# Parity of a long convolution's inner index on the partitions' halves, and two second stages in 64x64 blocks

## The chip, the cores and the metric

The kernel runs on one core of one Trainium2 chip. The metric is the device time of one launch in microseconds (us). The kernel before takes 2227.91 us, the median of three runs (2227.91, 2227.91 and 2229.37).

## The reference

Two layers follow one another. The first is a long convolution (a Hyena filter): with x and v of 4 batches x 12544 positions x 128 channels,

```python
h_filt = (np.maximum(pos_emb @ w1, 0.0) @ w2) * exp(-0.01 * pos)[:, None]
u  = x * v
y  = irfft(rfft(u, 2S) * rfft(h_filt, 2S))[:, :S]
x2 = x * y
```

The second is a feed-forward layer with a maximum of three products, `h = max(x2 @ w1, x2 @ w2, x2 @ w3)` and `h @ w_out`, with 128 channels and 768 hidden ones. All is fp32; the weights of the second layer arrive as 64-bit floats and are turned into fp32 on VectorE.

## The kernel before, in words

The transform of the convolution is split by hand into matrix products. A position is a block index (98 blocks for the signal, NH = 82 for the filter, whose window is zero after that) and an index s2 of 0 to 127 within the block. The **first stage** is a product over the blocks, which gives N1 = 90 complex frequencies for each s2 and channel. The **second stage** is a product over s2 with twiddles, frequency pair by frequency pair (NK = 45 pairs, called g). Signal and filter are then multiplied, and a third and a fourth product lead back. s2 is always split by its parity r: 2t+r with t of 0 to 63.

The work runs in four blocks of time. The instructions are issued in the order in which the program writes them (a manual schedule), one queue per engine, so an instruction that waits holds all that stands behind it on its engine.

**Loading and the filter's small network** (to 39.6 us). `pos_emb` is loaded in eight DMAs (L315) as two halves of the blocks (h = 0: blocks 0 to 40, h = 1: blocks 41 to 81) on two halves of the partitions. `mlp_in` (L346) multiplies by w1, `mlp_out` (L358) takes the maximum with zero and the window on VectorE and writes `hs`, which has 105 partitions: 41 blocks from partition 0 and 41 from partition 64. Between them stand the products of the first signal groups.

**First stages** (39.6 to 111.6 us). The loop over f (L1036) makes the first stage of the filter's 64 inner channels in 16 quads of four channels. `quad` calls `first_halves` (L170): for each channel, for each parity r and each half c of the table (real and imaginary part) one matmul of 105 partitions x 64 columns of weights x 90 columns, 16 per quad, and one ScalarE copy of 720 elements from PSUM into `specH`. Beside them VectorE multiplies x by v for signal groups 4 to 7 (`u_mul`, L384), TensorE turns them (`turn2`, L977), and `some` (L963) issues pieces of `convert` (L227), the 12 VectorE steps by which half of a weight matrix is turned from 64-bit floats into fp32; there are 8 such halves. `load_raw` (L214) fetches the next half by four DMAs on GpSimd's queue. After the 16 quads GpSimd copies four parts of the signal's spectrum that had been put `aside` (L1048), because `hs` lay on their place. Then the loop over u (L1050) does the same for signal groups 4 to 31, two at a time: two `quad`s of group u and u+1, one `turn2` of groups u+4 and u+5, and the loads (L379, on SyncE's queue) of u+10 and u+11. A `turn2` needs both products x*v of its groups. The PSUM tiles of this block are four, `acc`, taken in turn.

**The loop over frequency pairs of batch 0** (L1174, 111.6 to 279.6 us, NK + 3 = 48 steps). Step s holds:

- `s_second` (L1104): the filter's second stage, 4 matmuls of 128 x 64 x 128 columns into a PSUM tile of its own, and a ScalarE copy of 128 elements;
- `g_second` (L608): the signal's, 8 matmuls of 128 x 64 x 128 into another tile, and a ScalarE copy of 256 elements (`evens`);
- for the step before: `g_swap` (two ScalarE copies L627, L628) and `s_filter` (L1125), 16 matmuls of 64 x 64 x 128 that bring in w2, and a ScalarE copy of 1024 elements (L1151);
- for three steps before: `g_third` (L649), 8 matmuls of 128 x 64 x 128, a ScalarE copy (L660) and a store;
- for two steps before: the store of the filter's spectrum (`s_store`, on GpSimd's queue), the complex product `g_re`, `g_im` (two multiplications on VectorE, L633 and L637, and an addition on GpSimd, L638);
- for this step: `s_sums` (L1117, two sums of 128 elements on VectorE) and `butterfly` (L195, two sums of 256), both of even and odd parity;
- last on VectorE, `g_unfold` (L641, two sums L645), which waits for GpSimd's addition.

**Batches 1 to 3 and the second layer** (from 279.6 us). This fills the rest. The change does not touch it.

Of the kernel before, what the change touches and what calls it, by code (L numbers as in the profile page):

```python
# [42 lines left out]
def tables(NB):  # L43
# [11 lines left out]
    f1h = np.zeros((64 + HH, 2, 2 * N1))  # L55
    f1h[:HH, 0], f1h[64:, 0] = f1[:HH], f1[HH:NH]
    f1h[:HH, 1], f1h[64:, 1] = f1[HH:NH], f1[:HH]
# [11 lines left out]
    fwd = np.stack(half, 2)  # L69
# [26 lines left out]
def kernel(  # L96
# [53 lines left out]
    f1_sb = const.tile([NB, 2 * N1], FP32, name="f1")  # L150
    f1 = f1_sb[:]
# [18 lines left out]
    def first_halves(ps, lhs, table, dsts, engines):  # L170


        for i, a in enumerate(lhs):
            for r in range(2):
                for c in range(2):
                    nc.tensor.matmul(  # L176
                        ps[64 * c:64 * c + 64, 256 * i + r * N1:256 * i + (r + 1) * N1],
                        a[:, r, :], table[r][:, c * N1:(c + 1) * N1],
                        start=(i % 2 == 0 and r == 0), stop=True, skip_group_check=True)
        v = ps[:].rearrange("p (s m) -> p s m", m=256)[:, :, 0:2 * N1].rearrange(  # L180
            "p s (r k) -> p k r s", r=2)
        k0 = 0
        for dst, copy in zip(dsts, engines):
            k1 = k0 + dst.shape[1]
            copy(dst, v[:, k0:k1])
            k0 = k1

    def second(ps, w, g):

        for k in range(2):  # L190
            for r in range(2):
                halves_mm(ps[:, (2 * k + r) * D:(2 * k + r + 1) * D], w[:, k, r, :],
                          spec[:, 2 * g + k, r, :], k == 0 and r == 0, True)

    def butterfly(ps, eo, xs):  # L195
        v = ps[:, :].rearrange("p (k r d) -> p k r d", k=2, r=2)
        nc.vector.tensor_tensor(out=xs[:, :, 0, :], in0=eo[:], in1=v[:, :, 0, :], op=ALU.add)
        nc.vector.tensor_tensor(out=xs[:, :, 1, :], in0=eo[:], in1=v[:, :, 0, :],
                                op=ALU.subtract)

    def evens(ps, eo):
        v = ps[:, :].rearrange("p (k r d) -> p k r d", k=2, r=2)
        nc.scalar.copy(eo[:], v[:, :, 1, :])

# [19 lines left out]
    def convert(r, i, h):  # L227
# [6 lines left out]
        one = nc.vector.tensor_single_scalar  # L234
        tt = nc.vector.tensor_tensor
        ONE = 0x3F800000
# [3 lines left out]
            lambda: two(out=f2_, in0=lo, scalar1=9, scalar2=ONE,  # L240
                        op0=ALU.logical_shift_right, op1=ALU.bitwise_or),
            lambda: two(out=f1_, in0=hi, scalar1=12, scalar2=9,
                        op0=ALU.logical_shift_left, op1=ALU.logical_shift_right),
            lambda: one(f1_, f1_, ONE, op=ALU.bitwise_or),
            lambda: two(out=ex, in0=hi, scalar1=1, scalar2=21,
                        op0=ALU.logical_shift_left, op1=ALU.logical_shift_right),
            lambda: two(out=ex, in0=ex, scalar1=896, scalar2=0,
                        op0=ALU.subtract, op1=ALU.max),
            lambda: one(ex, ex, 255, op=ALU.min),
            lambda: one(ex, ex, 23, op=ALU.logical_shift_left),  # L250
            lambda: two(out=sg, in0=hi, scalar1=31, scalar2=31,
                        op0=ALU.logical_shift_right, op1=ALU.logical_shift_left),
            lambda: tt(out=ex, in0=ex, in1=sg, op=ALU.bitwise_or),
            lambda: one(f1f, f1f, 2.0 ** -20, op=ALU.subtract),
            lambda: nc.vector.scalar_tensor_tensor(
                out=f1f, in0=f2f, scalar=2.0 ** -20, in1=f1f, op0=ALU.mult, op1=ALU.add),
# [28 lines left out]
    w1_sb = sml.tile([P, FO], FP32, name="w1_sb")  # L285
    w2_in = sml.tile([P, D], FP32, name="w2_in")
# [10 lines left out]
    f1h = sml.tile([64 + HH, 2, 2 * N1], FP32, name="f1h")  # L297
# [6 lines left out]
    for h in range(2):  # L304
        nc.gpsimd.dma_start(
            win[64 * h:64 * h + HH],
            window[0, h * HH * P:(h + 1) * HH * P].rearrange("(n p) -> n p", p=P))
# [5 lines left out]
    for j, (lo_, hi_) in enumerate(zip(cuts, cuts[1:])):  # L313
        for h in range(2):
            (nc.scalar if (h + j) % 2 else nc.sync).dma_start(  # L315
                pos[64 * h:64 * h + 64, lo_ * P:hi_ * P],
                posT[:, (h * HH + lo_) * P:(h * HH + hi_) * P])
# [290 lines left out]
    def g_second(g):  # L608
        ps = state["cv"][1].tile([P, 512], FP32, tag="cv", name="ps2")
        second(ps, ws.pop((g, 0)), g)  # L610
        eo = state["cv"][0].tile([P, 2, D], FP32, tag="eo", name="eo", bufs=2)
        evens(ps, eo)
        pss[g], eos[g] = ps, eo

    def g_butterfly(g):
        if g % 3 == 2:
            xt = specH[:, 0:4].rearrange("p k r f -> p (k r f)").rearrange(
                "p (k r d) -> p k r d", k=2, r=2)
        else:
            xt = state["cv"][0].tile([P, 2, 2, D], FP32, tag="x", name="xt", bufs=state["xb"])  # L620
        butterfly(pss.pop(g), eos.pop(g), xt)
        xts[g] = xt

    def g_swap(g):
        xt = xts[g]
        xs = state["cv"][0].tile([P, 2, 2, D], FP32, tag="xs", name="xs", bufs=2)
# [3 lines left out]

    def g_re(g):
        xt = xts[g]
        nc.vector.tensor_tensor(out=xt[:], in0=xt[:], in1=hts[g][0][:], op=ALU.mult)  # L633

    def g_im(g, apart=False):
        xt, xs = xts[g], xss.pop(g)
        nc.vector.tensor_tensor(out=xs[:], in0=xs[:], in1=hts.pop(g)[1][:], op=ALU.mult)  # L637
        (nc.gpsimd if apart else nc.vector).tensor_tensor(  # L638
            out=xt[:], in0=xt[:], in1=xs[:], op=ALU.add)

    def g_unfold(g):  # L641
        y = xts.pop(g)
        ab = state["cv"][0].tile([P, 2, 2, D], FP32, tag="ab", name="ab", bufs=2)
# [756 lines left out]
```

## Time and profile before

| | |
|---|---|
| time, median of 3 runs | 2227.91 us |
| time of the profiled execution | 2221.21 us |
| its span, first to last instruction | 2219.4 us |
| granted TensorE clock, mean | 0.997 |
| TensorE matmul busy | 2194.1 us, 99% |
| VectorE busy | 1534.6 us, 69% |
| ScalarE busy | 1210.9 us, 55% |
| GpSimd busy | 1179.0 us, 53% |
| filter's first stage (16 quads and 2 turns) | 39.6 to 61.7 us |
| signal's first stage, groups 4 to 31 | 61.7 to 111.6 us |
| loop of batch 0 | 111.6 to 279.6 us |

How to read it: a time in the trace is counted from the start of the span. PE is TensorE's matmuls, PEld its weight loads, DVE VectorE, ACT ScalarE, POOL GpSimd, SPq SyncE's queue of DMA issues. The trace has two records for each fp32 matmul, so 16 matmuls show as x32. A busy TensorE is one that always had a matmul in flight; whether it was held up by others is seen only from what each engine waited for. L12 is line 12 of the kernel before.

### The profile page before, as it was taken

Reading aid. Unit: us, or ns where it says so; the run is one execution under the profiler, and the core shown is the slowest. Engines: PE = TensorE matmul, PEld = TensorE weight load, DVE = VectorE, ACT = ScalarE, POOL = GpSimd, SP = SyncE. Lnnn points to the kernel's source line nnn. Section 1 sums busy time; section 2 is a strip of 40 time slices with the busy share of each in tenths; the row PEclk is TensorE's granted clock in tenths of the full one; section 3 lists DMA queues with packets and bytes.
Section 4 is the critical chain, followed back from the end, with each engine's and each line's share of the span. In section 5 each row is a group of like instructions: output and inputs, shape, how many; then the busy total and the mean of one; then the engine's idle time right before and its main releaser. Section 6 shows DMA issues by size and latency. Waiting matters only on the chain.

```text
span 2219.4 us, 77166 instructions
## 1 busy us (share of the span) xinstructions
PE 2194.1 (99%) x31655; PEld 1297.3 (58%) x31655; DVE 1534.6 (69%) x3293; ACT 1210.9 (55%) x2223; POOL 1179.0 (53%) x1577
## 2 busy tenths in 40 slices
PE   9999999999999999999999999999999999999999
PEld 7988755555555455555555555555555545667776
DVE  5688857677877766667888766677878744554443
ACT  3699845466666555456666555556666622222222
POOL 1166567534455566544444566634454426666665
PEclk9999999999999999999999999999999999999999
DMA  8789999879999898879999999969999722222221
GB/s 196 186 264 311 291 181 196 171 191 233 247 246 241 218 188 175 168 175 245 230 256 231 229 195 178 173 158 252 236 240 238 200 79 58 59 71 69 63 58 24
DMA packets 491332, 411.62 MB, mean 185 GB/s; under 512 B 289406, under 2 KB 407920, under 8 KB 490979
## 3 DMA queue, kind: packets, MB, share of 16 engines
q1 hardware_dynamic: 443689, 274.50, 56.6%
q0 software_dynamic: 45808, 130.25, 21.5%
q8 instruction: 249, 4.08, 0.8%
q10 hardware_dynamic: 1482, 1.93, 0.4%
q14 instruction: 104, 0.85, 0.1%
HBM read 262.85 MB, written 84.67 MB: 157 GB/s over the span
## 4 chain that ended last, share of the span: by engine, by line
PE 84%; DMA 6%; DVE 3%; POOL 3%; issue 2%; SPq 1%; ACT 1%; POOLq 0%; DVEq 0%; ACTq 0%
PE hps L167 42%; PE ops L167 17%; PE ops L903 6%; PE cps L167 3%; PE cps L449 3%; PE ps L176 3%; PE cps L547 3%; PE cps L557 2%; DMA sq<-spec 2%; DMA ht<-hd 2%; DMA zt<-zd 1%; PE ps L167 1%; DMA wt<-wq_const 1%; POOL xt L638 1%; PE last L167 1%
## 5 line engine op out<-in xcount | busy, mean ns | idle before, releaser
L167 PE MATMUL hps<-gt,w_sb 128*64 128x392 f32 (+1 forms) x7672 | 1157.4, 495 | 0.8 <-DVE gt L829 0.7
L839 ACT ACTIVATE hid<-hps 128x392 f32<-128x392 f32 x768 | 382.5, 498 | 762.7 <-PE hps L167 744.9
L167 PEld LDWEIGHTS hps<-gt,w_sb 128*64 128x64 f32 (+1 forms) x7672 | 430.6, 126 | 439.1 <-issue 407.9
L842 DVE TENSOR_TENSOR hid<-hid,hps 128x392 f32<-128x392 f32 x768 | 427.8, 557 | 351.5 <-PE hps L167 335.8
L167 PE MATMUL ops<-hid,wo_sb 128*64 128x392 f32 x2304 | 476.9, 492 | 0.0
L599 POOL TENSOR_TENSOR cb<-cb,xs 128x512 f32<-128x512 f32 x135 | 177.4, 1314 | 404.9 <-DVE xs L596 389.5
L167 PEld LDWEIGHTS ops<-hid,wo_sb 128*64 128x64 f32 x2304 | 165.7, 137 | 213.5 <-issue 213.5
L572 DVE TENSOR_TENSOR cb<-cps,eo 128x512 f32<-128x512 f32 (+1 forms) x288 | 175.1, 649 | 72.8 <-ACT eo L569 71.7
L857 POOL DMA_DIRECT2D out_dram<-ot x96 | 76.3, 795 | 235.3 <-ACT ot L855 217.2
L587 ACT ACTIVATE xs<-cb 32x512 f32<-32x512 f32 x270 | 169.4, 628 | 21.5 <-DVE cb L572 12.6
L588 ACT COPY xs<-cb 32x512 f32<-32x512 f32 x270 | 166.3, 616 | 3.2
L603 DVE TENSOR_TENSOR xs<-cb 128x256 f32<-128x256 f32 x270 | 148.7, 598 | 6.5 <-POOL cb L599 6.5
L429 ACT COPY uT<-turned 113x512 uint16<-113x512 uint16 x180 | 126.0, 771 | 0.1
L386 POOL TENSOR_TENSOR ut<-ut 128x392 f32<-128x392 f32 x90 | 93.3, 1037 | 41.2 <-DMA ut<-in_vr_dram 39.2
L167 PEld LDWEIGHTS cps<-f4p,even 90*64 90x64 f32 x1552 | 87.2, 138 | 35.9 <-issue 33.2
L772 POOL DMA_DIRECT2D xT<-in_x_dram x172 | 101.1, 601 | 6.8 <-PE pt L1099 3.3
L580 POOL DMA_DIRECT2D zd<-cb x135 | 95.0, 704 | 14.6 <-DVE cb L572 10.7
L471 DVE TENSOR_TENSOR low<-high,cps 128x180 f32<-128x180 f32 x186 | 54.6, 334 | 67.6 <-ACT high L461 67.6
L928 POOL DMA_DIRECT2D out_dram<-o x120 | 72.5, 610 | 47.2 <-DVE o L921 45.7
L167 PE MATMUL cps<-f4p,zt 90*64 90x49 f32 x1552 | 95.8, 222 | 0.0
L547 PE MATMUL cps<-sq,wt 64*64 64x128 f32 x2160 | 90.6, 276 | 4.6 <-DMA wt<-wq_const 2.9
L413 POOL COPY planes<-ut 128x392 uint16<-128x392 uint16 x180 | 95.1, 564 | 0.0
(172 smaller groups left out, 3348.2 us busy)
## 6 DMA issues: line engine op xcount, KB each, us to landing
ht<-hd SPq DMA_DIRECT2D x264, 256.0 KB, 7.1
wt<-wq_const POOLq DMA_DIRECT2D x144, 256.0 KB, 5.3
zd<-cb POOLq DMA_DIRECT2D x135, 256.0 KB, 6.3
zt<-zd SPq DMA_DIRECT2D x384, 90.0 KB, 3.8
sq<-spec SPq DMA_DIRECT2D x528, 64.0 KB, 5.6
ut<-in_xr_dram SPq DMA_DIRECT2D x128, 196.0 KB, 4.3
ut<-in_vr_dram SPq DMA_DIRECT2D x128, 196.0 KB, 4.5
wt<-wt_const SPq DMA_DIRECT2D x90, 256.0 KB, 5.1
```

The lines of the kernel that those rows point to most:

```text
L167: nc.tensor.matmul(out[h:h + w], lhsT[:, h:h + w], rhs, start=start, stop=stop, skip_group_check=True)
L429: nc.scalar.copy(uts[u][0:HR, 8 * (u % 2):8 * (u % 2) + 8].rearrange("n s r t -> n (s r t)").bitcast(U16).rearrange("n (s r t h) -> n h s ...
L547: nc.tensor.matmul(ps[64 * a:64 * a + 64, at:at + D], w[64 * r:64 * r + 64, k, a, :], t[64 * r:64 * r + 64, k, :, a], start=(k == 0), stop ...
L572: nc.vector.tensor_tensor(out=cb[:, a, lo:hi], in0=ps[:, lo:hi], in1=eo[:, lo:hi], op=op)
L587: nc.scalar.mul(xs[at:at + 32], xt[at + 32:at + 64], -1.0)
L588: nc.scalar.copy(xs[at + 32:at + 64], xt[at:at + 32])
L599: nc.gpsimd.tensor_tensor(out=xts[g], in0=xts[g], in1=xs[:], op=ALU.add)
L603: nc.vector.tensor_tensor(out=ab[:, q], in0=y[:, 0], in1=y[:, 1], op=(ALU.subtract, ALU.add)[q])
L772: eng.dma_start(xT[c * NG:(c + 1) * NG].rearrange("d i p n -> d (i p) n"), x[:, 4 * i:4 * i + 8, c, b, :])
L839: nc.scalar.activation(h[:], pa[:, 0:N], Relu)
L842: nc.vector.tensor_tensor(out=h[:], in0=h[:], in1=pb[:, 0:N], op=ALU.max)
L903: nc.tensor.matmul(ps[32 * q:32 * q + 32, 0:H2], w[:, m:m + 32], rhs[:, H2 * c:H2 * c + H2], start=start, stop=True, skip_group_check=True)
```

## The change

Everything touches the first two blocks after loading and the loop of batch 0.

- `first_halves` now takes both halves of the table in one matmul (180 columns) and puts the parity r on the partitions' halves of the result: 8 matmuls per quad in place of 16. `spec` so holds r, not real and imaginary part, on its halves.
- The filter's quads are replaced by `filter_halves`. Its rows are now split by the parity p of the block index (partition 0: even blocks, partition 64: odd blocks; the loads of `pos_emb` and the window follow, in runs of 128 elements). Each half is multiplied apart, in 16 matmuls of 41 x 64 x 90, into the two banks of a PSUM tile. The sum and the difference of the two banks are the frequencies of both kinds. ScalarE copies one bank (360 elements) and VectorE makes both, or, in every second quad (`apart`), ScalarE copies both (720), VectorE makes the sum and GpSimd the difference. `eo` has one buffer for each of the two sizes.
- `u_mul` of the first and the second block moves from VectorE to GpSimd.
- `convert` has 10 VectorE steps in place of 12. Of the pieces, 8 are issued beside the filter's quads (44 before) and 6 in each turn of the loop over u (4 before). The next `load_raw` is issued after the sixth step of a conversion instead of before the first.
- In the loop `s_second` and `s_sums` are gone. `filter_second` (8 matmuls of 64 x 64 x 128) and `second` (16 of them) write one PSUM tile of two banks, followed by one ScalarE copy of 384 elements and two VectorE sums of 384. The filter's sums are so the last third of `xt`. PSUM is dealt anew: two tiles of two banks for this, one bank for `g_third`.
- After the loop the banks of `u_first` and `fold` are chosen from the new tiles.

```diff
 def first_halves(ps, lhs, table, dsts, engines):
     for i, a in enumerate(lhs):
         for r in range(2):
-            for c in range(2):
-                nc.tensor.matmul(
-                    ps[64 * c:64 * c + 64, 256 * i + r * N1:256 * i + (r + 1) * N1],
-                    a[:, r, :], table[r][:, c * N1:(c + 1) * N1],
+            nc.tensor.matmul(
+                ps[64 * r:64 * r + 64, 256 * i:256 * i + 2 * N1], a[:, r, :], table,
...
+def filter_halves(ps, f, apart):
+    for i in range(4):
+        for r in range(2):
+            for p in range(2):
+                b = 64 * (p ^ r)
+                nc.tensor.matmul(
+                    ps[64 * r:64 * r + 64, 512 * p + i * N1:512 * p + (i + 1) * N1],
+                    hs[b:b + HH, f + i, r, :], f1h[b:b + HH, r, :],
+                    start=(i == 0), stop=True, skip_group_check=True)
+    v = ps[:].rearrange("p (a m) -> p a m", a=2)[:, :, 0:4 * N1]
+    dst = specH[:].rearrange("p (k x) c f -> p x k c f", x=2)[..., f:f + 4]
+    n = 1 + apart
+    eo = sml.tile([P, n, 4 * N1], FP32, tag=f"eo{n}", name="eo")
+    nc.scalar.copy(eo[:], v[:, 2 - n:])
+    def turned(m):
+        return m.rearrange("p (s c k) -> p k c s", s=4, c=2)
+    for x, op in enumerate((ALU.add, ALU.subtract)):
+        eng, e_ = (nc.gpsimd, eo) if x and apart else (nc.vector, v)
+        eng.tensor_tensor(out=dst[:, x], in0=turned(e_[:, 0]), in1=turned(eo[:, n - 1]), op=op)
...
 def second(ps, w, g):
     for k in range(2):
-        for r in range(2):
-            halves_mm(ps[:, (2 * k + r) * D:(2 * k + r + 1) * D], w[:, k, r, :],
-                      spec[:, 2 * g + k, r, :], k == 0 and r == 0, True)
+        for c in range(2):
+            for r in range(2):
+                for h in range(2):
+                    nc.tensor.matmul(
+                        ps[64 * h:64 * h + 64, 512 * r + k * D:512 * r + (k + 1) * D],
+                        w[64 * r:64 * r + 64, k, c, 64 * h:64 * h + 64],
+                        spec[64 * r:64 * r + 64, 2 * g + k, c, :],
+                        start=False, stop=True, skip_group_check=True)
+def filter_second(ps, w, g):
+    for c in range(2):
+        for r in range(2):
+            for k in range(2):
+                nc.tensor.matmul(
+                    ps[64 * k:64 * k + 64, 512 * r + 2 * D:512 * r + 3 * D],
+                    specH[64 * r:64 * r + 64, 2 * g + k, c, :],
+                    w[64 * r:64 * r + 64, k, c, :],
+                    start=(c == 0), stop=True, skip_group_check=True)
...
 for f in range(0, FO, 4):
-    quad([hs[:, f + i] for i in range(4)], (f1h[:, 0], f1h[:, 1]), specH[:, :, :, f:f + 4])
+    filter_halves(next(turns_), f, f // 4 % 2 == 1)
     u, k = divmod(f // 4, 4)
     if u < 2:
         if k in (0, 1):
-            u_mul(2 * u + 4 + k)
+            u_mul(2 * u + 4 + k, nc.gpsimd)
...
-    some(2 if u < 2 and k < 2 else 3)
+    some(f // 4 % 2)
...
 def g_second(g):
-    ps = state["cv"][1].tile([P, 512], FP32, tag="cv", name="ps2")
-    second(ps, ws.pop((g, 0)), g)
-    eo = state["cv"][0].tile([P, 2, D], FP32, tag="eo", name="eo", bufs=2)
-    evens(ps, eo)
+    ps = qps.tile([P, 1024], FP32, tag="q", name="ps2")
+    w = ws.pop((g, 0))
+    filter_second(ps, w, g)
+    second(ps, w, g)
+    eo = cvp.tile([P, 3 * D], FP32, tag="eo", name="eo", bufs=2)
+    nc.scalar.copy(eo[:], ps[:, 512:512 + 3 * D])
...
 def g_butterfly(g):
...
+    for x, op in enumerate((ALU.add, ALU.subtract)):
+        nc.vector.tensor_tensor(out=xt[:, x], in0=eo[:], in1=ps[:, 0:3 * D], op=op)
```

In the order that the changed program gives each engine, GpSimd's queue around the filter's quads reads: x*v of groups 0 to 4, difference of quad 1, x*v of 5, difference of quad 3, x*v of 6, difference of 5, x*v of 7, differences of 7, 9, 11 and 13, one `load_raw` (four DMAs), difference of 15, the four copies from `aside`, x*v of groups 8 to 11, a `load_raw`, x*v of 12 to 15, a `load_raw`, x*v of 16 to 18, a `load_raw`, and so on.

## The prediction

> **What bounds the kernel now.** First the stretches: the busy time of each engine in the filter's first stage, in the signal's first stage, in the steady part of the loop, and in one stretch near the loop's end (start:end and length, busy us of PE, PEld, DVE, ACT, POOL with counts, granted clock, DMA share, GB/s).
>
> ```profile
> 39.60:61.70 22.10, 22.10 (x532) 21.52 (x530) 21.13 (x56) 14.58 (x20) 8.65 (x16) 1.00 0.63 159
> 61.70:111.60 49.90, 48.87 (x998) 45.22 (x994) 28.16 (x68) 33.85 (x41) 3.91 (x6) 1.00 0.79 195
> 136.00:166.00 30.00, 30.00 (x648) 26.88 (x644) 26.56 (x71) 29.30 (x55) 20.49 (x27) 1.00 0.96 316
> 266.90:273.80 6.90, 5.90 (x68) 4.83 (x72) 6.83 (x16) 5.09 (x8) 2.04 (x4) 0.51 0.67 186
> ```
>
> In the first two TensorE never stops: they are bound by it. In the loop TensorE and ScalarE are both full and VectorE nearly, so there the order of time must be read. Two of VectorE's turns, with GpSimd's:
>
> ```profile
> 160.91 0.76 DVE L645 TENSOR_TENSOR ab<-xt 128x256 f32<-128x256 f32 x2 [0.40 <-POOL xt L638]
> 161.59 0.69 DVE L633 TENSOR_TENSOR xt<-xt,ht 128x512 f32<-128x512 f32 x1
> 162.19 0.68 DVE L637 TENSOR_TENSOR xs<-xs,ht 128x512 f32<-128x512 f32 x1
> ...
> 163.03 1.27 POOL L638 TENSOR_TENSOR xt<-xt,xs 128x512 f32<-128x512 f32 x1 [1.12 <-DVE xs L637]
> ```
>
> Unfold, two products, GpSimd's addition, unfold again: 0.68 + 0.60 + 0.84 + 1.30 from start to start = 3.42 us, and VectorE stands idle 0.40 us waiting for GpSimd, while `s_sums` and `butterfly` fit into the addition's time. The chain of waits says the same: from 125 to 220 us it is made of L638, L645, L637 and again L638, three steps in 10.2 us. So a step takes 3.40 us, by that ring; ScalarE's six instructions add up to 3.37 and TensorE's four groups to 3.35.
>
> Then the rows that price the filter's new form: the quads now, the conversions' loads and the copies from `aside`.
>
> ```profile
> L176 PE MATMUL ps<-f1h,spec 105*64 105x90 f32 x512 | 20.5, 241 | 0.0
> L386 POOL TENSOR_TENSOR ut<-ut 128x392 f32<-128x392 f32 x90 | 93.3, 1037 | 41.2 <-DMA ut<-in_vr_dram 39.2
> L1048 POOL COPY spec<-wo_sb 128x256 f32<-128x256 f32 x3 | 1.7, 596 | 2.5 <-PE ps L176 2.5
> ```
>
> **The change, part by part.**
>
> *Start.* `pos_emb` comes in runs of 512 B where it came in 5 KB. Packets of 392 B (x and v) and of 5 KB both move about 14 to 15 B/ns per DMA engine in this trace, so the cost lies between 0 and 2 us; I take 0.9, as TensorE waits for the last piece (first matmul at 16.39). Against it, x*v of groups 0 and 1 no longer stand behind `mlp_out` on VectorE, where TensorE lost 0.4 us at 24.2. Together **+0.5**.
>
> *Filter's quads on TensorE.* A quad has 32 records, in pairs 16 x 0.0775 = 1.24 us (16 quads and two turns: 22.1). The new matmuls go four at a time, as `u_products` does (L449, 49x64x90: 32 records in 0.82 us with the switch of shape), so 8 x 0.0775 = 0.62 us: 9.9 us are taken from TensorE. What is late next is the other engines, and here the time is decided.
>
> *GpSimd's queue.* It gets eight differences of 360 elements. The nearest rows of the same operation, 1271 ns for 512 and 1037 for 392, give 1.95 ns an element, so 0.975 us. But its operands are read with a step of 90 elements and written in runs of four; the row with such runs is L1048's copy, 0.52 to 0.73 us for 256 from one operand, so two operands at 2.03 ns each are 1.46. Between 0.975 and 1.46, one row sharing the operation and the other the pattern, I take the middle, 1.2. Row first: no GpSimd instruction here reads with such a step. [...]
>
> The queue up to the x*v of groups 8 and 9, which `turn2(8)` needs: 8 x 1.2 + 3 x 1.03 (x*v of 5, 6, 7) + 2.2 (`load_raw`, the 2.25 us of L219's four issues) + 4 x 0.63 (copies) + 2 x 1.03 = 19.5 us. It can't begin before ScalarE has made the first copy of both banks: ScalarE is done with its older work at 40.96, copies 0.46 and 0.76 (rows of 360 and 720 elements), so 42.3. And `eo` has one buffer: where no x*v or load stands between two differences, each waits for the next copy, 0.92 us with the handovers, three times: 2.8. At the two turns it waits for TensorE: x*v of 5 (then 7) ends, half a turn 0.49, switch 0.17, quad 0.62, drain 0.25, copy 0.76, handover 0.1: 2.4 us, twice. So the queue is through at 42.3 + 19.5 + 2.8 + 4.8 = 69.4, and `turn2(8)` at 69.9. Before, that turn ended at 65.3 (64.33 + 0.98). TensorE itself would be there at about 63, so it stands for some 6 us: **+4.6** in place of a gain (+2.8 at 0.975 us, +6.7 at 1.46).
>
> *After it.* 12 turns of the loop over u at 2 x 1.22 + 1.16 = 3.60 us in place of 3.64 (8 matmuls of 180 columns are 8 x 0.1525): **-0.5**. GpSimd now has 2.06 us of x*v in each, and three more `load_raw`: from group 10 to 19, 10 x 1.03 + 3 x 2.2 = 16.9 us for five turns of 3.6 = 18, and VectorE's conversions, which it meets all this time, stretched L1048 from 0.53 to 0.73; I take 0.1 each, which uses the slack up where a landing stands between: 0 to 2, I take **+1.0**.
>
> *Clock.* After an idle TensorE the last row of the first fence shows half clock (0.51) for 6.9 us; the 16 matmuls of `s_filter` there took 1.98 us where they take 1.10. The wait of 6 us at `turn2(8)` is longer than the one of 1.99 us that came before that stretch. One such half-clock window costs half of its 3.4 us, the filter's quads at 65% busy may add one more: 0 to 3.4, I take **+1.7**. [...]
>
> *The loop.* ScalarE loses one instruction (0.28 + 0.37 become some 0.48), VectorE two (0.48 + 0.74 become 1.0), TensorE keeps its passes: 8 + 16 matmuls, four at a time at 0.109 per group, are 1.31 us as before, with two switches of shape a step as before. The ring of 3.40 us has the same instructions as before, in shapes that the later batches run (L591, L596, L599, same medians), and what VectorE saves is saved inside GpSimd's 1.27 us: **0**. If it did not hide there, a step would gain the 0.2. Only the four steps with a turn, which ScalarE fills (4.43 us, from copy L1151 at 239.07 to the next at 243.51), gain about 0.18: **-0.7**. The filter's sums now end with `butterfly`; TensorE reaches `s_filter` at about the same time, so this wait costs nothing while TensorE keeps 0.05 us of room a step. VectorE's move of x*v and two conversion steps less are free: VectorE has 20 us of room in the second stretch.
>
> Sum: 0.5 + 4.6 - 0.5 + 1.0 + 1.7 - 0.7 = **+6.6**, so 2227.8 against the profiled execution's 2221.2 (span 2219.4 and 1.8 around it), and 2227.9 + 6.6 = **2234.5** against the median, which lies 6.7 us above the profiled one.
>
> **Rivals.** *Cheap GpSimd*: differences at 0.975, no half clock, no shortage later: 0.5 + 2.8 - 0.5 - 0.7 = +2.1, 2230.0. For it: rows of the same operation; against it: the step of the reads. *TensorE stays the bound* (faster): GpSimd reaches x*v of 9 before TensorE needs it. Then `turn2(8)` comes 9.9 us sooner: 0.5 - 9.9 - 0.5 - 0.7, 2217.3. It decides from the point where the queue's 69.4 falls to 65 and below, that is at differences of 0.6 us or less, or if the copies and the load stood elsewhere; against it, no row has them so cheap. *Dear blocks*: GpSimd at 1.46, 3.4 us of half clock and 2 of shortage: +0.5 + 6.7 - 0.5 + 2 + 3.4 - 0.7 = +11.4, 2239.3; or TensorE needs 0.1 us more for the 24 matmuls of a step, which its 0.05 of room lets through for some 40 steps: +2 on the forecast. *It does not do what it says*: matmuls from two row halves into one bank don't run together, a quad stays at 1.24 us. Then TensorE would take 22 us again and GpSimd's last copy, mult and turn come on top; also about 2239. `mlp_in` does that in groups of four, so I give it little.
>
> **How the numbers follow.** Forecast 0.45 (2231 to 2237.5), cheap GpSimd 0.25 (2228 to 2231), dear blocks with the last rival 0.20 (2237 to 2241), faster 0.10. The measurement tells 0.2%, 4.5 us, from no change: below 2223.5 is faster, above 2232.4 slower. Slower: most of the forecast (0.41) and all of the dear, 0.61; faster 0.09; the rest 0.30. The range 2227 to 2240 leaves out the faster case and the end of the dear one.
>
> **What would show it.** Right: a pause of 4 to 7 us on TensorE before the turn of groups 8 and 9, ended by GpSimd's x*v; the filter's 16 quads in about 10 us of busy time; GpSimd's differences at 1.0 to 1.5 us; a half-clock stretch after it; the loop's step still 3.40 us with VectorE idle for 0.5 before L645's successor. Wrong: no pause there, a step of the loop below 3.35 or above 3.45, or the signal's stage not back at 3.6 us a turn.

## The result, and the profile after

The changed kernel takes 2261.3 us (median of four executions, 2252.2 to 2267.0) where the kernel before takes 2228.2 beside it (2227.9 to 2229.4): 1.0144 times as long, 95% interval 1.0102 to 1.0186. The forecast had the sign, with 2234.5 us and a range of 2227 to 2240; the loss is five times the one forecast. The profiled execution took 2255.8 us, with a span of 2254.1, 34.7 more than the 2219.4 before. By stage, from the two traces:

| | before | after | difference |
|---|---|---|---|
| first matmul of the filter's quads | 39.6 | 40.6 | +1.0 |
| end of the turn of groups 8 and 9 | 65.3 | 75.3 | +10.0 |
| end of the first stage (last signal quad) | 110.6 | 125.1 | +14.6 |
| loop, from the first ScalarE copy of the filter's product to the 43rd | 146.9 us | 160.1 us | +13.2 |
| from there to VectorE's first even part of the next stage | 24.9 us | 24.9 us | 0 |
| all that follows | 1931.3 us | 1938.1 us | +6.8 |

The first two rows lie within the third; the small gap between first stage and loop gives 0.1 more. The same stretches as before, in the busy time of each engine (same columns): the filter's first stage, the signal's, and 30 us of the loop.

```profile
40.60:66.20 25.60, 21.95 (x530) 19.92 (x529) 19.23 (x27) 11.71 (x20) 13.11 (x10) 0.59 0.32 77
66.20:125.10 58.90, 54.32 (x548) 43.97 (x544) 57.09 (x78) 33.71 (x41) 37.67 (x48) 0.89 0.80 191
146.00:176.00 30.00, 28.50 (x778) 24.87 (x779) 25.10 (x52) 26.39 (x42) 19.80 (x26) 1.00 0.96 294
```

TensorE was full or nearly so in all three before. Now it has gaps in all three, its clock was 0.59 and 0.89 in the first two, and in the second VectorE is busy for 57.1 of 58.9 us, twice what it was, although it lost the products x*v. The rows that the forecast priced, from 40 to 126 us (busy, then mean ns of one):

```profile
L412 POOL TENSOR_TENSOR ut<-ut 128x392 f32<-128x392 f32 x27 | 27.9, 1062 | 0.9 <-DMA ut<-in_vr_dram 0.8
L210 DVE TENSOR_TENSOR specH<-ps,eo 128x360 f32<-128x360 f32 x24 | 18.3, 813 | 7.5 <-ACT eo L203 7.5
L195 PE MATMUL ps<-f1h,spec 41*64 41x90 f32 x512 | 18.3, 333 | 0.0
L210 POOL TENSOR_TENSOR specH<-eo 128x360 f32<-128x360 f32 x8 | 11.9, 1484 | 20.5 <-ACT eo L203 20.4
```

GpSimd's difference takes 1.48 us, at the upper of the two bounds. VectorE's sum takes 0.81, or 0.72 from one start to the next, which the forecast had not priced.

In the loop, an undisturbed step. VectorE's turn (unfold, two products, the sums), then the chain of waits:

```profile
188.04 0.76 DVE L682 TENSOR_TENSOR ab<-xt 128x256 f32<-128x256 f32 x2 [0.55 <-POOL xt L675]
188.72 0.68 DVE L669 TENSOR_TENSOR xt<-xt,ht 128x512 f32<-128x512 f32 x1
189.32 0.68 DVE L673 TENSOR_TENSOR xs<-xs,ht 128x512 f32<-128x512 f32 x1
189.92 1.01 DVE L653 TENSOR_TENSOR xt<-eo,ps 128x384 f32<-128x384 f32 x2
```

```profile
184.24 0.60 PE ps L231 x16
184.84 0.87 PE ps L219 x32
185.71 0.87 PE sps L1140 x32
186.58 1.02 PE ps L169 x16
187.60 0.60 PE ps L231 x16
```

VectorE still waits for GpSimd, 0.55 us where it was 0.40, but the chain has left that ring: four groups of TensorE, 3.36 us, are the step. Such steps are as long as forecast (3.37). But 17 of the 31 steps from the fourth on, ahead of those with a turn, are longer than 3.5 us, up to 5.2, and what TensorE waited for in them is for the most part in no engine's records (the three largest rows: line that waited, waited for: us in total, times, longest):

```profile
PE sps L1140 <- issue: 3.1, 3, 1.4
PE ps L169 <- issue: 2.3, 2, 1.4
PE ps L219 <- issue: 1.9, 3, 0.8
```

"issue" means that nothing shown released it. Smaller rows name VectorE (1.0 us) and ScalarE (0.6 us). The kernel before had no "issue" row in its loop.

### The profile page after: what moved, and what is told of

The parts are those of the page before. It is cut to its first block, busy times and chain, and to the rows that moved or that the text cites. A ratio compares the mean times of both kernels' runs of the same rounds, so it can differ in the third digit from the quotient of the medians.

```text
span 2254.1 us, 78230 instructions
## 1 busy us (share of the span) xinstructions
PE 2205.7 (98%) x32223; PEld 1276.7 (57%) x32223; DVE 1556.5 (69%) x3179; ACT 1207.0 (54%) x2178; POOL 1225.6 (54%) x1617
## 4 chain that ended last, share of the span: by engine, by line
PE 76%; DMA 12%; DVE 5%; issue 3%; SPq 2%; POOL 1%; ACT 1%; ACTq 0%; DVEq 0%; POOLq 0%
PE hps L169 37%; PE ops L169 14%; PE ops L939 6%; DMA sq<-spec 4%; DMA ht<-hd 4%; PE cps L169 3%; PE cps L475 3%; PE cps L573 2%; PE ps L169 2%; PE cps L583 2%; PE sps L1140 2%; PE ps L219 2%; DMA wt<-wq_const 1%; SPq L546 1%; PE ps L231 1%
## 5 line engine op out<-in xcount | busy, mean ns | idle before, releaser
L169 PEld LDWEIGHTS hps<-gt,w_sb 128*64 128x64 f32 (+1 forms) x7672 | 420.4, 126 | 448.2 <-issue 411.1
L598 DVE TENSOR_TENSOR cb<-cps,eo 128x512 f32<-128x512 f32 (+1 forms) x288 | 175.2, 650 | 72.2 <-ACT eo L595 71.5
L613 ACT ACTIVATE xs<-cb 32x512 f32<-32x512 f32 x270 | 169.5, 628 | 21.2 <-DVE cb L598 12.4
L412 POOL TENSOR_TENSOR ut<-ut 128x392 f32<-128x392 f32 x122 | 126.6, 1044 | 70.4 <-DMA ut<-in_vr_dram 70.1
L573 PEld LDWEIGHTS cps<-sq,wt 64*64 64x64 f32 x2160 | 65.9, 132 | 54.6 <-issue 43.8
```

The costliest lines, as they stand in the source:

```text
L169: nc.tensor.matmul(out[h:h + w], lhsT[:, h:h + w], rhs, start=start, stop=stop, skip_group_check=True)
L412: eng.tensor_tensor(out=a[:], in0=a[:], in1=v[:], op=ALU.mult)
L573: nc.tensor.matmul(ps[64 * a:64 * a + 64, at:at + D], w[64 * r:64 * r + 64, k, a, :], t[64 * r:64 * r + 64, k, :, a], start=(k == 0), stop ...
L598: nc.vector.tensor_tensor(out=cb[:, a, lo:hi], in0=ps[:, lo:hi], in1=eo[:, lo:hi], op=op)
L613: nc.scalar.mul(xs[at:at + 32], xt[at + 32:at + 64], -1.0)
```

## The experiments

**The theory for the loop: TensorE runs out of instructions.** Laid side by side, the weight loads and the packets of the DMA queue named "instruction" show a pattern. The 12 such stalls of over 0.5 us are 126 to 128 matmul records apart, or a multiple of that, whichever line is then at work, and each ends 1.3 to 1.6 us after the end of a packet of 16 KB. The loop has 32 such packets and 4064 records, 127 a packet. A few of them:

```
stall (us)          records since the last    last packet on the instruction queue
200.77 to 201.85    126                       199.43 to 200.39
206.52 to 207.03    127                       204.35 to 205.70
235.41 to 236.68    127                       234.25 to 235.23
250.43 to 252.25    380                       249.94 to 250.89
257.07 to 258.15    127                       255.47 to 256.55
```

One such stall stands in the trace of the kernel before, ahead of its loop, among the matmuls of the filter's small network:

```profile
24.62 0.57 PE L353 MATMUL ps<-w_sb,specH 64*41 64x64 f32 x13 [0.39 <-issue]
```

The weight loads pause there from 23.93 to 24.62 us, and the pause ends 1.52 us after the end of a packet. The same load comes late in all eleven variants below, by 0.3 to 1.0 us and 1.3 to 1.6 us after a packet, whether VectorE or GpSimd makes x*v of groups 0 and 1. In the changed kernel's own trace, at half clock from 17.9 to 24.8 us, it does not.

The change raised a step's matmul records from 72 to 96 (8 + 16 became 16 + 32 in the second stages). At 3.37 us a step a packet's worth then lasts 4.5 us where it lasted 6.0, and the DMA engines that bring it are 0.9 to 1.0 full with data (0.96 in the 30 us of the loop above). Rivals: the shared banks, the new order, the blocks themselves. **The theory for the first stage:** GpSimd and VectorE hold each other up, and the waits at the turns bring a half clock. Rival: the work of VectorE or GpSimd itself is too long.

**All x*v of the first stage back on VectorE.**

```diff
-                u_mul(u, nc.gpsimd)
+                u_mul(u)
...
-                u_mul(2 * u + 4 + k, nc.gpsimd)
+                u_mul(2 * u + 4 + k)
...
-                u_mul(u + 4 + v, nc.gpsimd)
+                u_mul(u + 4 + v)
```

> All of the first stage's x*v go back to VectorE; the rest is the changed kernel. Theory (VectorE and GpSimd hold each other up): in the changed kernel the conversion's instruction that meets a batch of x*v on GpSimd takes 3.6 to 5.8 us where the same one takes 0.36 alone, and GpSimd's loads of the next raw weights wait for VectorE in turn. Without the batches that instruction falls to 0.4 to 0.6 us, the turns of the u loop come back from 4.15 to 3.6 to 3.7 us, and the last quad of the first stage ends at 117 to 121 us in place of 125.2; the total falls by 4 to 8. Rival (the first stage is late because of the filter's differences and the half clock alone): the u loop stays at 4.0 us or more a turn and the stage ends at 123 or later. The loop after it keeps its stalls either way.

2251.0 us, 1.0121 (1.0104 to 1.0138) of the kernel before. The first stage ends at 120.2 us, within the theory's range. First the changed kernel, VectorE and then GpSimd in the u loop (some rows of VectorE between those shown are left out), then this variant's VectorE:

```profile
79.65 4.63 DVE L266 TENSOR_SCALAR ta<-raw 128x384 int32<-128x384 int32 x1
84.32 0.36 DVE L267 TENSOR_SCALAR ta<-ta 128x384 f32<-128x384 int32 x1
87.96 3.64 DVE L266 TENSOR_SCALAR ta<-raw 128x384 int32<-128x384 int32 x1
```

```profile
78.06 2.02 POOL L247 DMA_DIRECT2D raw<-in_moe_w_dram  x4 [1.65 <-DVE tb L277]
80.10 3.96 POOL L412 TENSOR_TENSOR ut<-ut 128x392 f32<-128x392 f32 x4
86.37 2.01 POOL L247 DMA_DIRECT2D raw<-in_moe_w_dram  x4 [2.32 <-DVE tb L277]
```

```profile
78.08 0.56 DVE L412 TENSOR_TENSOR ut<-ut 128x392 f32<-128x392 f32 x1
78.56 0.35 DVE L266 TENSOR_SCALAR ta<-raw 128x384 int32<-128x384 int32 x1
```

In the changed kernel VectorE's conversion step starts at 79.65 and ends at 84.28, just after GpSimd's four products (80.10 to 84.06); alone it takes 0.35. GpSimd in its turn waits for VectorE before each load. So the two take turns. From the turn of groups 8 and 9 on, the u loop takes 47.1 us here, 49.8 in the changed kernel and 45.3 before, so this costs 2.7 of the 4.5 us lost there; eight of ten turns are back at 3.6 to 3.7 us, two take 4.2 and 4.5. But the turn of groups 8 and 9 itself ends at 73.1, only 2.2 sooner. TensorE now waits for VectorE's x*v at the turns before it (2.2 and 1.8 us), and the half clock comes as well (from 44.0 to 71.3 us): GpSimd's queue alone was not what the filter's stage hung on.

**The loop's third stage in 128 columns.**

```diff
-                halves_mm(ps[:, (2 * k + q) * D:(2 * k + q + 1) * D], w[:, k, q, :],
-                          ab[:, k, q, :], k == 0 and q == 0, True)
+                nc.tensor.matmul(ps[:, (2 * k + q) * D:(2 * k + q + 1) * D], w[:, k, q, :],
+                                 ab[:, k, q, :], start=k == 0 and q == 0, stop=True, ...)
```

> The loop's third stage in four matmuls of 128 columns in place of eight of 64; the rest is the changed kernel. Theory (TensorE runs out of instructions): the loop's stalls on TensorE lie 127 or 128 matmuls apart or a multiple, and end 1.3 to 1.6 us after the end of an instruction-queue packet of 16 KB. A step falls from 96 to 88 matmul records, a packet's instructions last 4.9 us in place of 4.5 at full pace, so fewer stalls: from the first copy of the filter's product to the last in the loop 146 to 154 us in place of 160.1, and a total 6 to 14 lower. Rival (the stalls come from the shared banks, from the waits of the new order or from the 64x64 blocks): the loop stays at 158 to 162 us.

**A fourth of the loop's data left out.**

```diff
-            ws[s - 3, 1] = wi.pop(s - 3)
+            ws[s - 3, 1] = wi[(s - 3) % 3]
...
-            if s < NK:
-                wi[s] = load_dir(s, 1)
```

> Leaves out the loads of the inverse direction's constants from the fourth step of the loop on (256 KB of about 1.05 MB a step); those of the first three steps are used again, so the numbers of the output are not the reference's. TensorE's instructions are the same. Theory (instruction packets come late because they stand behind data on full DMA engines): DMA share in the loop falls from 0.95 to about 0.75, the packets land earlier and the stalls on TensorE vanish or nearly: 145 to 150 us from the first copy of the filter's product to the last in place of 160.1, total 9 to 15 lower. Rival (the stalls come from the order of the step, the banks or the blocks): 157 to 162 us.

**The third stage in more matmuls.**

```diff
+                for n in range(0, D, 64):
-                halves_mm(ps[:, (2 * k + q) * D:(2 * k + q + 1) * D], w[:, k, q, :],
-                          ab[:, k, q, :], k == 0 and q == 0, True)
+                    halves_mm(ps[:, (2 * k + q) * D + n:(2 * k + q) * D + n + 64], w[:, k, q, :],
+                              ab[:, k, q, n:n + 64], k == 0 and q == 0 and n == 0, True)
```

> The loop's third stage in sixteen matmuls of 64x64 outputs in place of eight of 64x128: the same product, 16 records more a step (112 in place of 96), the rest is the changed kernel. Theory (TensorE runs out of instructions): a packet's 128 records last 3.9 us at full pace, and nearly every packet is waited for: the loop takes 172 to 195 us from the first copy of the filter's product to the last in place of 160.1. Rival (only busy time and the data's waits count): 160 to 169, at most 0.2 us a step for the shorter matmuls.

**The signal's second stage in 128 columns.**

```diff
-                    for h in range(2):
-                        nc.tensor.matmul(ps[64 * h:64 * h + 64, ...],
-                            w[64 * r:64 * r + 64, k, c, 64 * h:64 * h + 64], ...)
+                    nc.tensor.matmul(ps[:, ...], w[64 * r:64 * r + 64, k, c, :], ...)
```

> The signal's second stage in eight matmuls of 128 columns in place of sixteen of 64 (the halves of the rows stay apart); the rest is the changed kernel. 80 records a step in place of 96, so a packet of instructions lasts 5.4 us at 3.37 us a step; before it was 6.0 us with 72 records and no stall, with 88 records 5 stalls were left, with 96 there were 12, with 112 some 22. Theory (TensorE runs out of instructions): 0 to 3 stalls at the end of a packet, 147 to 151 us from the first copy of the filter's product to the 43rd, in place of 160.1 (before: 146.9). Rival (the loop loses by the order of the new step or its banks, and fewer instructions help only where the matmuls get shorter): 154 us or more.

**The kernel before, in more matmuls** (its second and its third stage, by the same edit as above).

> The kernel before, with the loop's second and third stages in matmuls of 64 output columns in place of 128: the same products, 104 records a step in place of 72, no block of 64x64, no new order, no new bank. Theory (TensorE runs out of instructions): a packet's 128 records last 4.3 us at full pace, so stalls at the ends of packets appear here too: 8 to 20 of them, and 158 to 172 us from the first copy of the filter's product to the 43rd in place of 146.9. Rival (the stalls belong to the new step): none, and 147 to 153 us, up to 0.12 us a step for the shorter matmuls.

These five go together. The stalls are counted where a gap of over 0.5 us between the starts of two weight loads ends 1.15 to 1.75 us after the end of an instruction packet; their sum is of these gaps less the usual 0.06 us, and "rest" is the loop without them. The "issue" rows add up to less, 7.9 us in the changed kernel, since they count from the modelled end of the matmul in flight.

| | records a step | DMA share | loop, us | stalls | their sum | rest | time against before |
|---|---|---|---|---|---|---|---|
| before | 72 | 0.94 | 146.9 | 0 | 0 | 146.9 | |
| second stage wide | 80 | 0.94 | 159.1 | 0 | 0 | 159.1 | 1.0146 (1.0117 to 1.0175) |
| third stage wide | 88 | 0.94 | 157.3 | 4 | 5.5 | 151.8 | 1.0131 (1.0110 to 1.0152) |
| changed kernel | 96 | 0.93 | 160.1 | 12 | 12.6 | 147.5 | 1.0144 (1.0102 to 1.0186) |
| fewer loads | 96 | 0.81 | 153.1 | 7 | 6.9 | 146.3 | 1.0085 (1.0064 to 1.0106) |
| before, split | 104 | 0.88 | 171.5 | 16 | 19.0 | 152.5 | 1.0102 (1.0085 to 1.0119) |
| third stage split | 112 | 0.86 | 181.0 | 24 | 28.8 | 152.1 | 1.0224 (1.0204 to 1.0244) |

The number of stalls follows the number of records, over both kernels. The kernel before, with neither blocks nor new order nor new banks, gets 16 of them by being cut into more matmuls; the trace puts them down as in the changed kernel (here up to 262 us, the loop goes on to 287):

```profile
PE ps L167 <- issue: 6.4, 10, 1.8
PE sps L1137 <- issue: 3.4, 4, 1.1
```

One of the 16 the trace puts down to VectorE's x*v. The changed kernel's loop, unaltered, ran in six of the profiles: 160.1 to 169.3 us with 12 to 15 stalls, of which the one above is the shortest. Less data with the same instructions leaves seven, so the packets do wait behind data; that as many are left at a share of 0.81 was more than expected. Three of the expectations in time missed: 153.1 lies between theory and rival, and so does 157.3, because the third stage in 128 columns costs 3.43 us a step undisturbed, and because its longest stall was followed by a half clock (238.3 to 241.7 us). (One such stretch of 3.4 us also lies in the rest of "before, split", and two in that of "third stage split".) The second stage in 128 columns took every stall away, as the theory said, but the loop stayed at 159.1, on the rival's side. Why, TensorE's own row shows:

```profile
176.67 1.16 PE L218 MATMUL ps<-spec,wt 64*128 64x128 f32 x16
177.76 1.10 PE L1139 MATMUL sps<-w2x,xt 64*64 64x128 f32 x32
178.79 1.09 PE L169 MATMUL ps<-ab,wt 128*64 128x128 f32 x16
179.82 0.67 PE L230 MATMUL ps<-wt,specH 64*64 64x128 f32 x16
```

The group takes 1.09 us from start to start where four blocks of 64x64 at a time took 0.87, and `s_filter` behind it 1.03 in place of 0.87: as in the kernel before, where it took 1.03 as well, the group ahead of it has another shape. Every step between the first three and those with a turn is 3.75, without one stall. The rest of the changed kernel's loop, 147.5 us, is within 0.6 of the kernel before: order, banks and blocks cost next to nothing, the stalls 12.6 of the 13.2 us.

128 matmul records with their loads are 256 instructions. The spacing of 126 to 128 records puts about that many into a packet of 16 KB, and the whole run agrees with it: its 254 packets on that queue would so hold 65,024 instructions where TensorE has 64,446 records. How many packets TensorE holds at a time, no run here tells.

**x*v of groups 4 to 9 early** (those of groups 0 to 3 are VectorE's again as well, not shown).

```diff
+    for u in range(4, 8):
+        u_mul(u, nc.gpsimd)
     for f in range(0, FO, 4):
...
-            if k in (0, 1):
-                u_mul(2 * u + 4 + k, nc.gpsimd)
+            if k == 1:
+                u_mul(8 + u, nc.gpsimd)
...
-            if u + 4 < NU:
-                u_mul(u + 4 + v, nc.gpsimd)
+            if 10 <= u + 4 + v < NU:
+                u_mul(u + 4 + v)
```

> The changed kernel with x*v of groups 4 to 7 on GpSimd ahead of the filter's first quad (it is idle there for 10 us), of 8 and 9 behind the second and the sixth quad, and all later ones on VectorE. Theory (TensorE's waits at the turns behind GpSimd's differences start the half clock, and half clock plus the queue make the filter's stage long): no wait at the first two turns, the clock stays at 1.0 or falls for less than 10 us, the turn of groups 8 and 9 ends at 62 to 68 us in place of 75.3 (73.1 with all x*v on VectorE), and the first stage at 109 to 115 in place of 125.1 and 120.2. Rival (VectorE's 24 sums at 0.74 us and the conversions bound the stage at 1.25 us a quad whatever the clock is): the turn of 8 and 9 ends at 69 or later, the first stage at 116 or later.

The turn of groups 8 and 9 ends at 66.6 us and the first stage at 113.4, both as the theory had it; the half clock came in two stretches, 47.8 to 51.3 and 58.1 to 64.9 us, 10.2 us where less than 10 was expected. In the changed kernel TensorE's row had shown how it starts, with the stretch of half clock below it:

```profile
45.50 1.09 PE L417 MATMUL ps<-eye,ut 128*98 128x128 f32 x4 [2.21 <-POOL ut L412]
46.52 5.08 PE L195 MATMUL ps<-f1h,spec 41*64 41x90 f32 x128
...
54.13 1.09 PE L417 MATMUL ps<-eye,ut 128*98 128x128 f32 x4 [1.44 <-POOL ut L412]
55.16 11.11 PE L195 MATMUL ps<-f1h,spec 41*64 41x90 f32 x288
66.20 5.07 PE L177 MATMUL ps<-f,uT 98*64 98x180 f32 x32
73.01 1.09 PE L417 MATMUL ps<-eye,ut 128*98 128x128 f32 x4 [1.74 <-POOL ut L412]
```

```profile
45.20:79.40 34.20, 30.52 (x496) 25.79 (x498) 29.20 (x41) 13.39 (x19) 22.45 (x25) 0.50 0.33 82
```

Three quads before the first wait took 2.09 us, 0.70 each; nine after it 11.1, 1.23 each. Two waits of 2.2 and 1.4 us at the turns, four signal quads of 2.3 to 2.5 us in place of 1.3, a third wait at the turn of 8 and 9. Yet the total is 2250.6 us, 1.0090 (1.0066 to 1.0114): the loop of this execution had 15 stalls and took 168.0.

**Reads in order.**

```diff
-            return m.rearrange("p (s c k) -> p k c s", s=4, c=2)
+            return m.rearrange("p (k c s) -> p k c s", s=4, c=2)
```

> The filter's sums and differences read their operands in the order in which they lie in place of a step of 90 elements; they write the same pattern, so the filter's spectrum gets its columns in another order and the output isn't the reference's. Prices the step of the reads: if GpSimd's 1.48 us come from the reads, a difference falls to 0.9 to 1.1 us (the 1.95 ns an element of its other additions and products) and VectorE's sum from 0.74 to about 0.5; if the runs of four that are written cost it, both stay within 0.1.

```profile
L210 DVE TENSOR_TENSOR specH<-ps,eo 128x360 f32<-128x360 f32 x24 | 11.9, 524 | 11.6 <-ACT eo L203 11.5
L210 POOL TENSOR_TENSOR specH<-eo 128x360 f32<-128x360 f32 x8 | 7.6, 950 | 21.8 <-ACT eo L203 21.8
```

0.95 us in place of 1.48 and 0.52 in place of 0.81: the step of the reads is all of it, 56% on GpSimd and 55% on VectorE, and the written runs of four cost GpSimd nothing beside the 0.975 us of its other rows. (The row of L1048's copies, which gave the forecast 1.46 us, came near.) And yet its nine quads at half clock took 11.1 us again, with VectorE idle for 3.5 of the 11.1 us: there TensorE at half clock sets the pace. This execution ends at 2265.6, with a turn at 71.5 and a first stage at 124.1.

**Positions in long runs.**

```diff
-                posT[:, 0:NH * P].rearrange("f (n h p) -> f h n p", h=2, p=P)[:, h, lo_:hi_])
+                posT[:, (h * HH + lo_) * P:(h * HH + hi_) * P].rearrange("f (n p) -> f n p", p=P))
```

> The loads of the positions' embedding in the old long runs (5 KB in place of 512 B), rows in the old order, so the output isn't the reference's; the rest is the changed kernel. Theory: the last piece landed at 17.4 to 18.3 us in the changed kernel and four variants with the same loads, at 16.3 before, and TensorE's first product of it waits for it; it comes back to 16.2 to 16.6 and the first product to 16.3 to 16.8. Rival (the landing is late by chance or because of other loads): 17.4 or later.

The last piece shown landed at 16.2 us, TensorE's first product of it is at 16.68 (16.39 before, 18.15 in the changed kernel, 17.4 to 19.7 in the other variants with the short runs) and the filter's first matmul at 38.9. So the runs of 512 B cost 0.7 to 3 us at the start, 1.5 in the changed kernel; the total of one execution, 2259.3, can't show that.

**A mended first stage**: early x*v, and the filter's matmuls write each bank in the order in which the sums read it (the sums' reads are edited as in the experiment on them). Then the same with the third stage in 128 columns.

```diff
-            f1h[b:b + HH, r] = np.concatenate([t.real, t.imag], 1)
+            f1h[b:b + HH, r] = np.stack([t.real, t.imag], 2).reshape(HH, N1)
...
-                        ps[64 * r:64 * r + 64, 512 * p + i * N1:512 * p + (i + 1) * N1],
+                        ps[64 * r:64 * r + 64, 512 * p + i:512 * p + 4 * N1:4],
```

> The version with early x*v, and the filter's matmuls write their bank in the order in which the sums read it (outputs with a step of four elements, the table's columns reordered to match). Theory: VectorE's sums fall to 0.52 us and GpSimd's differences to 0.95, TensorE at full clock needs 0.70 us a quad, and the half clock doesn't come or is short; the turn of groups 8 and 9 ends at 58 to 63 us in place of 66.6 and the first stage at 104 to 109 in place of 113.4 (before: 110.6). The loop keeps its stalls, 157 to 170 us; total 3 to 9 below the version with early x*v. Rival (outputs with a step slow the matmuls, or TensorE's own half clock sets the pace whatever VectorE does): the turn ends at 65 or later.

> The same, with the loop's third stage in four matmuls of 128 columns (88 records a step in place of 96). Theory: first stage as in the mended version, the loop 153 to 160 us, total 4 to 12 below the mended version; against the kernel before 4 to 8 are gained in the first stage and 6 to 13 lost in the loop, so it does not get below it. Rival (the stalls have another cause than the number of instructions): the loop as long as in the mended version.

The mended version takes 2247.9 us, 1.0078 (1.0059 to 1.0097), and with the wide third stage 2242.1, 1.0046 (1.0031 to 1.0061). The sums cost 0.52 and 0.95 us, and the turn ends at 62.9 and 64.3. Outputs with a step of four elements cost TensorE nothing: the first three quads take 2.09 us, as without it. The next four take 3.02, 0.3 us of it in one pause of the weight loads:

```profile
42.09 1.08 PE L417 MATMUL ps<-eye,ut 128*98 128x128 f32 x8
43.09 3.02 PE L195 MATMUL ps<-f1h,spec 41*64 41x90 f32 x128
...
53.59 3.35 PE L195 MATMUL ps<-f1h,spec 41*64 41x90 f32 x113 [1.43 <-issue]
56.88 5.06 PE L177 MATMUL ps<-f,uT 98*64 98x180 f32 x32
```

The first stage ends at 109.0 us in the one and, with the same code up to there, at 112.1 in the other; before it was 110.6. Even this filter stage, the densest in instructions of all (32 matmul records in 0.70 us), has a stall at the end of a packet (1.43 us) and a half clock behind it. The loops had 13 stalls (162.0 us) and 10 (159.6). The first is 2.7 us below the version with early x*v, just short of the 3 expected and within the spread of both. The second is 5.8 us below the first, nearer to the lower end of what was expected; the 4 to 8 us that the first stage was to gain on the kernel before were 1.6 in the one and a loss of 1.5 in the other. Neither gets below the kernel before: the loop gives away several times what the mended first stage gains.

## Why the prediction was wrong

- **The loop: 0 forecast for the steps, +13.2 measured, and 13 to 22 over the six profiles of this loop.** This is the step that failed. The forecast counted TensorE's passes ("8 + 16 matmuls, four at a time ... are 1.31 us as before") and never its instructions: 24 matmuls of 64x64 do in nearly the same time what 12 did, and TensorE emptied its packets faster than they came. In busy time the forecast was near: the two groups take 0.60 + 0.87 = 1.47, 0.16 more than 1.31, and `s_filter`, now behind a group of its own shape, 0.87 in place of 1.03; undisturbed steps are at 3.37. VectorE's idle time before the unfold is 0.55 (0.5 forecast). The -0.7 for the four steps with a turn was small too: two that no stall met took 4.37 us in place of 4.43, 0.06 each and not 0.18. The loop before shows no stall of this kind, so it gave no price; the rows that could have raised the question are the "instruction" queue of the profile and the "issue" at 24.62 us, which the forecast read as VectorE's x*v.
- **The turn of groups 8 and 9: +4.6 forecast, +9.0 measured behind the start's 1.0.** The mechanism was right in part: a pause, ended by GpSimd's x*v, was there, of 1.7 us, but two more of 2.2 and 1.4 us lay at the turns before it, where the forecast had counted waits for GpSimd's queue and not for TensorE. The difference took 1.48 us, not 1.2. That queue alone did not decide: with x*v taken off it the turn came only 2.2 us sooner. VectorE had got "20 us of room in the second stretch" and its new sums in the first no price at all; they take 0.72 us each from start to start, some 1.25 us a quad with the conversion steps, as long as a quad before.
- **The clock: 1.7 forecast, bound 3.4.** The half clock lasted 34.2 us. The forecast took half of one window of 3.4 us (the trace before has such stretches, from 17.8 to 21.2 and from 290.8 to 294.3 us); that the filter's quads might add a second was its estimate. But in all eight executions that ran nine filter quads on end at half clock, 11.1 us, these never brought the clock back. What it cost alone can't be told from VectorE's pace in the filter's stage, as each limits a quad to 1.23 to 1.25 us. What the two mends are worth can: the turn ends at 75.3 us with neither, 71.5 with reads in order, 66.6 with early x*v and 62.9 with both. So early x*v, with the half clock that it spares, is worth 8.6 to 8.7 us and the order of the reads 3.7 to 3.8, by one execution each.
- **After the turn: +1.0 and -0.5 forecast, +4.5 measured.** GpSimd's shortage came, and with it what the forecast had seen only as a stretched copy of 0.1 us each: a conversion step of VectorE that meets a batch of three to five of GpSimd's products ends only when the batch is over, after 3.6 to 5.8 us, five times in the u loop: it ends 0.2 to 0.4 us after the batch each time, and the step at 79.65, 4.63 us long here, takes 0.35 alone.
- **The start: +0.5 forecast, +1.0 measured at the filter's first matmul.** The cause was the one named, and dearer: TensorE's first product of the last piece came 1.8 us later, where 0.9 was forecast. The 0.4 us set against it was not VectorE's: that pause ends behind an instruction packet, and it stays in the variants where GpSimd makes these x*v.
- **The rest: +6.8 us that the change doesn't own.** The same code after the loop took 1930.6 to 1943.8 us in the thirteen profiles, and 1939.5 in the variant of the kernel before, whose code there is the same. It differs from execution to execution; the profiled execution before was a short one, 2221.2 us against a median of 2227.9. What makes it differ is open, and there is no second profile of the kernel before.
- **The rivals.** Cheap GpSimd and TensorE as the bound are refuted by 1.48 us and by the waits. Dear blocks came nearest, with the bounds on GpSimd right; but its price for the loop, +2 us of TensorE's time, was the wrong mechanism. That the quads don't do what they say is refuted: 0.70 us at full clock, 0.62 forecast.

## What to carry to other kernels

Count the instructions of an engine as a resource of their own: in these loops, with DMA engines 0.81 to 0.94 full, cutting TensorE's work into more and smaller matmuls at equal busy time was free only while a packet of instructions (128 matmul records with their loads) lasted long enough for the next one to arrive (6.0 us was enough, 5.0 and less was not). Before moving work between VectorE and GpSimd, look at what runs on the other at that moment (a conversion step of 0.35 us took 4.63 here), and price the access pattern that each operand is read with, on both engines (0.81 us against 0.52, 1.48 against 0.95). A short TensorE wait ahead of small matmuls can cost far more than itself: here 34.2 us at half clock began at one of 2.2 us, and 11.1 us of the filter's matmuls did not end them.

## What the runs showed of the hardware that was not expected

- TensorE stopped at the end of a packet of 16 KB of its instructions in the loops whose matmul records came at 128 in about 5 us or less, with the DMA engines 0.81 to 0.94 full: 12 times in the changed kernel's loop, for 0.5 to 1.8 us. In the loops at 128 in 6 us (a share of 0.94) there was no such stall.
- The granted clock stayed at half through 11.1 us of matmuls of 41 x 64 x 90 without a pause in the trace, in eight executions. It came back 3.7 to 5.4 us after signal quads (98 x 64 x 180) began in five executions; in six others, the changed kernel's among them, a wait for x*v followed the first two such quads (5.1 us), and it came back only 10 to 13.5 us after they began. These matmuls fill 41 of 64 rows of each block; whether that keeps the clock down was not tested.
- Reading with a step of 90 elements cost GpSimd 56% (1.48 us against 0.95) and VectorE 55% (0.81 against 0.52); TensorE's outputs with a step of four elements cost nothing more, 2.09 us for three quads with and without it.
